# Attention and expert network on one core: the network folded into one 32x128 matrix a batch

## The chip, the cores and the metric

The kernel runs on one core of a Trainium2 chip. The metric is device time in microseconds of one execution. Engines: PE (TensorE: matmuls, transposes), DVE (VectorE), ACT (ScalarE), POOL (GpSimd) and SP (SyncE, which here issues the DMAs).

## The reference

For each of four batches of 11456 tokens with 128 features: 32 inducing vectors attend to all tokens, which gives `h` (32 rows), and the tokens attend to `h`. Then each token of the result goes to the one of eight experts whose vector it is nearest to, and through that expert's two-layer network (128 to 1024 to 128, ReLU), times the probability of that expert.

```python
def mab(q, kv):
    s = scale * (q @ kv.transpose(0, 2, 1))
    s = s - s.max(-1, keepdims=True)
    a = np.exp(s)
    a /= a.sum(-1, keepdims=True) + 1e-09
    return a @ kv
h = mab(I, x)
return mab(x, h).astype(np.float32)
...
    logits = xn @ en.T / tau
    expert_idx = np.argmax(logits, axis=1)
    ...
        h = np.maximum(x[mask] @ w1[e], 0.0)
        out[mask] = gate_w[mask, None] * (h @ w2[e])
```

A token's attended vector is a mix of the 32 rows of `h` with positive weights. Where the 32 rows' products with a column of `w1` are nearly equal, the sign of the mix is the sign of their sum, whatever the weights.

## The kernel before

A batch's tokens are cut into seven superblocks (`SBS`): five of four groups, one of two, one short one; a group is 512 tokens, four tiles of 128. A batch goes through two stages.

First stage (`stage1`): scores of the inducing vectors (`s1_pe`, four column strips of PE, L252), running maximum and exponentials (`s1_max` L265, `s1_exp` L282), transposes (`t1_pe` L297, `t1_copy` L303), products with the tokens into `h` (`h_pe` L310). `finish`, `table` and `guess` normalise `h`, make its table and choose the expert that most of the batch's tokens go to; `load_w` loads that expert's weights.

Second stage (`stage2`): scores against `h` (L252), copy (L478), transposes (L483), maximum, exponentials (L487 to L493), a split into float16 parts (`pst`, L496 to L499), transposes back into `pT` (L506). `norms` (L531, L542) gives squared lengths and logits, `gate` (L562 to L608) the factor of each token, which goes through memory (`gd`) to be spread over partitions (`gb`).

The network (`ffn`) goes over all groups of 512 tokens in eight chunks of the hidden layer. One step is one chunk:

```python
nc.tensor.matmul(ps[:, :w], lhsT=st.G[:K3, P * ch:P * ch + P], rhs=st.pT[k][:K3, w * t:w * t + w], start=True, stop=True)
nc.scalar.activation(hi[:, :w], ps[:, :w], AF.Relu)
nc.vector.scalar_tensor_tensor(lo[:, :w], ps[:, :w], 0.0, hi[:, :w], ALU.max, ALU.subtract)
```

and three matmuls with the second layer's parts `wh` and `wl` (L797, L798, L806). So a step is four matmuls of 512 columns, one ACT and one DVE instruction of 128x512. `G` is the first layer's weights times `h`. Attention runs as generators (`Clock`, `attention`) between the steps, 56 steps ahead of the network; the order is fixed by `FRAME` and the lags at the top of the file. Tokens of other experts than the batch's are redone in a loop at the end (`worklist` writes the list `items`; the loop reads it).

Of the kernel before, what the change touches and what calls it, by code (L numbers as in the profile page):

```python
# [83 lines left out]
def tile_attn_moe(ctx: ExitStack, tc: tile.TileContext, xT, xP, xR, indT, emb, tau, w1, w2, aux, outT):  # L84
    nc = tc.nc
    pool = lambda name, bufs, **kw: ctx.enter_context(tc.tile_pool(name=name, bufs=bufs, **kw))
    const = pool("const", 1)
# [13 lines left out]
    ps_acc = pool("ps_acc", 2, space=PSUM)
    ps_att = pool("ps_att", ATT_BUFS, space=PSUM)
    dram = pool("dram", 7, space=DRAM)
    keep = pool("keep", 1, space=DRAM)

    held = [0]

    def take():
        """A bank of attention's. It's given back (done) when all that reads it has been issued."""
        held[0] += 1  # L110
        assert held[0] <= ATT_BUFS
        return ps_att.tile([P, 512], F32, name="att")

    def done():
        held[0] -= 1

    def att():
        while held[0] >= ATT_BUFS:
            yield 1
        return take()  # L120

# [1 line left out]
    wz = const.tile([P, 512], F16, name="wz")  # L123
    nc.vector.memset(wz, 0.0)
    ident = const.tile([P, P], F32, name="ident")
    make_identity(nc, ident)
    ident16 = const.tile([P, P], F16, name="ident16")
    nc.vector.tensor_copy(ident16, ident)
    # sel4[(j, m), (r, m')] = 1 where m == m'
    sel4 = const.tile([P, 4, M], F32, name="sel4")  # L130
    for j in range(4):
        for r in range(4):
            nc.vector.tensor_copy(sel4[32 * j:32 * j + 32, r, :], ident[32 * j:32 * j + 32, 32 * j:32 * j + 32])
    ones = const.tile([P, P], F32, name="ones")
    nc.vector.memset(ones, 1.0)
    rev = const.tile([P, E], F32, name="rev")
    for e in range(E):
        nc.vector.memset(rev[:, e:e + 1], float(E - e))
    half = const.tile([P, 16], F32, name="half")
    nc.vector.memset(half, 0.5)  # L140

    indT_sb = const.tile([P, M], F32, name="indT_sb")
    nc.sync.dma_start(indT_sb, indT)
    emb_sb = const.tile([E, P], F32, name="emb_sb")
    itau = const.tile([P, 1], F32, name="itau")

    enT = const.tile([P, E], F32, name="enT")

    def load_small():
        nc.sync.dma_start(emb_sb, emb)  # L150
        nc.sync.dma_start(itau, tau.broadcast_to([P, 1]))
        nc.sync.dma_start(ax, aux)

    def experts():
        """The experts' vectors, normalised, transposed; in three parts."""
        nc.vector.reciprocal(itau, itau)
        esq = const.tile([E, P], F32, name="esq")
        ess = const.tile([E, 1], F32, name="ess")
        nc.scalar.activation(esq, emb_sb, AF.Square, accum_out=ess)
        nc.gpsimd.tensor_tensor(ess, ess, half[:E, 0:1], ALU.pow)  # L160
        yield
        nc.vector.tensor_scalar_add(ess, ess, 1e-6)
        nc.vector.reciprocal(ess, ess)
        nc.vector.tensor_scalar_mul(emb_sb, emb_sb, ess)
        yield
        tp = take()
        nc.tensor.transpose(tp[:, 0:E], emb_sb, ident[:E, :E])
        nc.vector.tensor_copy(enT, tp[:, 0:E])
        done()
        yield  # L170

    def squares(src, w):
        """The sums of the squares of src's rows."""
        junk = work.tile([P, 512], F32, name="junk")
        ss = small.tile([P, 1], F32, name="sq", bufs=6)
        nc.scalar.activation(junk[:, :w], src, AF.Square, accum_out=ss)
        return ss

    def pow2(sums):
        """A power of two, on every partition: times 2 ** -66 it takes the root of all the sums' sum  # L180
        to within [1 / 3, 1]."""
        ps = yield from att()
        for i, a in enumerate(sums):
            nc.tensor.matmul(ps[:, 0:1], lhsT=ones, rhs=a, start=i == 0, stop=i == len(sums) - 1)
        yield 1
        m1 = small.tile([P, 1], F32, name="m1")
        nc.vector.tensor_scalar_max(m1, ps[:, 0:1], 1e-30)
        done()
        # The exponent halved and negated: 2 ** (65 - (exponent + 1) // 2).
        m2 = small.tile([P, 1], F32, name="m2", bufs=4)  # L190
        nc.vector.tensor_scalar(m2.bitcast(I32), m1.bitcast(I32), 1, 0x7F800000, ALU.logical_shift_right, ALU.bitwise_and)
        nc.vector.tensor_scalar(m2.bitcast(I32), m2.bitcast(I32), 0x7F800000, None, ALU.bitwise_xor)
        return m2

    def scaled(m2, top, by, name):
        sc = small.tile([P, 1], F32, name=name, bufs=2)
        nc.vector.scalar_tensor_tensor(sc, m2, top * 2.0 ** -66, by, ALU.mult, ALU.mult)
        return sc

    def split_rows(dst, src, sc, odd):  # L200
        """dst[(hi, lo, hi, lo) x 32, w] of src (four equal blocks of rows) times sc. odd is sc in
        the blocks of lo and 0 in the others."""
        nc.scalar.activation(dst, src, AF.Copy, scale=odd)
        yield 1
        nc.vector.scalar_tensor_tensor(dst, src, sc, dst, ALU.mult, ALU.subtract)

    ax = const.tile([NB * E, 2 * NB * E + 2], F32, name="ax")
    onec = const.tile([P, 1], F32, name="onec")
    nc.vector.memset(onec, 1.0)

    par = const.tile([P, 1], F32, name="par")
    for q in range(4):
        nc.vector.memset(par[32 * q:32 * q + 32], float(q % 2))
    zcol = const.tile([P, 1], F16, name="zcol")
    for q in range(4):
        nc.vector.memset(zcol[32 * q:32 * q + 32], float(1 - q % 2))

    # What a second visit of a batch needs, and the experts that each batch's tokens go to.
    kT = keep.tile([NB, P, P], F32, name="kT")
# [897 lines left out]
```

## Time and profile before

| | |
|---|---|
| three runs | 841.62, 843.49 (median), 845.50 us |
| span of the profiled execution | 841.2 us |
| PE, DVE, ACT, POOL busy | 815.0 (97%), 702.9 (84%), 645.9 (77%), 182.7 us (22%) |
| DMA | 96.00 MB, mean 114 GB/s |

The span goes from the first to the last instruction of one profiled execution; no time of its own is given for that execution beside it, and the three runs lie 0.4 to 4.3 us above it. "Busy" is the union of an engine's instructions. Matmul ends are modelled, so distances between starts are the safer reading for PE.

### The profile page before, as it was taken

Reading aid. Unit: us, or ns where it says so; the run is one execution under the profiler, and the core shown is the slowest. Engines: PE = TensorE matmul, PEld = TensorE weight load, DVE = VectorE, ACT = ScalarE, POOL = GpSimd, SP = SyncE. Lnnn points to the kernel's source line nnn. Section 1 sums busy time; section 2 is a strip of 40 time slices with the busy share of each in tenths; the row PEclk is TensorE's granted clock in tenths of the full one; section 3 lists DMA queues with packets and bytes.
Section 4 is the critical chain, followed back from the end, with each engine's and each line's share of the span. In section 5 each row is a group of like instructions: output and inputs, shape, how many; then the busy total and the mean of one; then the engine's idle time right before and its main releaser. Section 6 shows DMA issues by size and latency. Waiting matters only on the chain.

```text
span 841.2 us, 15737 instructions
## 1 busy us (share of the span) xinstructions
PE 815.0 (97%) x5286; PEld 395.7 (47%) x5286; DVE 702.9 (84%) x1674; ACT 645.9 (77%) x1894; POOL 182.7 (22%) x388
## 2 busy tenths in 40 slices
PE   9899899999999999999999999999999999999994
PEld 5544445444544444444454444444454444444442
DVE  5587787987989889898898898888888988898983
ACT  4588768786887887877688878878688888888662
POOL 0034411221122222312022222222112222223100
PEclk9999999999999999999999999999999999999998
DMA  8534151422633324241663244132311122212221
GB/s 331 215 143 151 52 197 55 159 90 95 122 150 138 121 106 176 73 162 53 95 221 145 80 153 164 64 140 106 99 64 58 39 85 80 64 51 89 63 81 35
DMA packets 32091, 96.00 MB, mean 114 GB/s; under 512 B 5257, under 2 KB 7665, under 8 KB 27265
## 3 DMA queue, kind: packets, MB, share of 16 engines
q1 hardware_dynamic: 32000, 94.91, 33.1%
q8 instruction: 44, 0.72, 0.4%
q14 instruction: 47, 0.38, 0.2%
HBM read 70.84 MB, written 24.05 MB: 113 GB/s over the span
## 4 chain that ended last, share of the span: by engine, by line
PE 87%; DVE 3%; DMA 3%; ACT 3%; issue 1%; POOL 1%; SPq 1%; ACTq 0%; POOLq 0%
PE hps L783 18%; PE acc L797 17%; PE acc L806 17%; PE acc L798 17%; PE att L252 5%; PE att L531 3%; DMA w2t<-in_w 3%; PE att L310 2%; PE att L506 2%; PE att L297 1%; PE att L483 1%; ACT hi L785 1%; DVE lo L786 1%; ACT junk L542 1%; PE hps L874 1%
## 5 line engine op out<-in xcount | busy, mean ns | idle before, releaser
L786 DVE SCALAR_TENSOR_TENSOR lo<-hps,hi 128x512 f16<-128x512 f32 (+1 forms) x736 | 482.9, 671 | 77.9 <-ACT hi L785 71.7
L785 ACT ACTIVATE hi<-hps 128x512 f16<-128x512 f32 (+1 forms) x736 | 429.4, 589 | 110.0 <-PE hps L783 107.6
L783 PE MATMUL hps<-pT,G 96*128 96x512 f16 (+1 forms) x736 | 275.6, 375 | 1.4 <-DVE lo L786 0.7
L797 PE MATMUL acc<-hi,wh 128*128 128x512 f16 (+1 forms) x736 | 275.2, 374 | 0.3 <-DVE o L817 0.3
L806 PE MATMUL acc<-lo,wh 128*128 128x512 f16 (+1 forms) x736 | 273.6, 372 | 0.0
L798 PE MATMUL acc<-hi,wl 128*128 128x512 f16 (+1 forms) x736 | 273.4, 371 | 0.0
L562 POOL TENSOR_TENSOR nrm<-ss,half 128x4 f32<-128x4 f32 (+1 forms) x92 | 93.3, 1014 | 241.6 <-ACT junk L542 241.6
L542 ACT ACTIVATE junk<-att 128x128 f32<-128x128 f32 (+1 forms) x368 | 99.5, 286 | 15.8 <-PE att L531 11.9
L798 PEld LDWEIGHTS <-wl 128*128 128x128 f16 x736 | 72.2, 98 | 83.0 <-issue 1.8
L806 PEld LDWEIGHTS <-wh 128*128 128x128 f16 x736 | 70.7, 96 | 83.7 <-issue 0.4
L783 PEld LDWEIGHTS <-G 96*128 96x128 f16 x736 | 71.3, 97 | 81.3 <-issue 22.8
L797 PEld LDWEIGHTS <-wh 128*128 128x128 f16 x736 | 72.4, 98 | 58.9 <-issue 5.6
L542 ACT ACTIVATION_READ_ACCUMULATOR junk<-att 128x1 f32 (+1 forms) x368 | 78.7, 215 | 0.0
L817 DVE SCALAR_TENSOR_TENSOR o<-acc,cO,gb 128x512 f32<-128x512 f32 (+1 forms) x92 | 66.9, 727 | 0.9 <-DMA gb<-gd 0.4
L510 ACT COPY pT<-att 96x512 f16<-96x512 f16 (+1 forms) x90 | 48.9, 550 | 7.1 <-PE att L506 6.7
L531 PEld LDWEIGHTS <-pT 96*128 96x128 f16 (+1 forms) x368 | 29.6, 97 | 34.8 <-issue 13.2
L531 PE MATMUL att<-hst,pT 96*128 96x137 f16 (+1 forms) x368 | 45.1, 224 | 0.1
L497 POOL TENSOR_SCALAR pst<-pst 128x512 f16<-128x512 f16 (+2 forms) x28 | 15.2, 544 | 111.0 <-ACT pst L496 111.0
L506 PEld LDWEIGHTS <-pst 128*96 128x96 f16 (+1 forms) x368 | 26.2, 123 | 10.9 <-issue 1.7
L506 PE MATMUL att<-ident,pst 128*96 128x128 f16 (+1 forms) x368 | 28.1, 218 | 0.9 <-POOL pst L497 0.9
L252 PE MATMUL att<-xTt,hT 128*32 128x512 f32 (+1 forms) x192 | 28.0, 569 | 0.1
L543 DVE COPY raw<-att 128x27 f32<-128x27 f32 (+4 forms) x140 | 24.1, 174 | 3.8 <-ACT junk L542 2.3
(188 smaller groups left out, 635.3 us busy)
## 6 DMA issues: line engine op xcount, KB each, us to landing
gb<-gd SPq DMA_DIRECT2D x88, 256.0 KB, 3.4
out<-o SPq DMA_DIRECT2D x43, 512.0 KB, 4.4
xTt<-in_xT SPq DMA_DIRECT2D x20, 1024.0 KB, 7.1
xt<-in_xP SPq DMA_DIRECT2D x17, 1024.0 KB, 9.5
xTt<-in_xT SPq DMA_DIRECT2D x4, 512.0 KB, 11.4
w1t<-in_w SPq DMA_DIRECT2D x8, 256.0 KB, 3.0
w2t<-in_w SPq DMA_DIRECT2D x4, 512.0 KB, 5.8
xt<-in_xP SPq DMA_DIRECT2D x3, 512.0 KB, 12.4
```

The source lines that it names most:

```text
L252: nc.tensor.matmul(ps[32 * j:32 * j + 32, :ng * w].rearrange("p (g i) -> p g i", i=w), lhsT=lhsT, rhs=v[:, j], start=True, stop=True)
L506: nc.tensor.transpose(tp[:K3, w * t:w * t + w], pst[:w, 8 * c + t].rearrange("p q m -> p (q m)"), ident16[:w, :w])
L531: nc.tensor.matmul(v[:w, t - 3 * c], lhsT=st.pT[k][:K3, t * w:t * w + w], rhs=st.hst[:K3], start=True, stop=True)
L542: nc.scalar.activation(junk[:w, :C], v[:w, t, :C], AF.Square, accum_out=st.ss[k][:w, a:a + 1])
L562: nc.gpsimd.tensor_tensor(nrm[:, a:a + pw], ss[:, a:a + pw], half[:w, a:a + pw], ALU.pow)
L783: nc.tensor.matmul(ps[:, :w], lhsT=st.G[:K3, P * ch:P * ch + P], rhs=st.pT[k][:K3, w * t:w * t + w], start=True, stop=True)
L785: nc.scalar.activation(hi[:, :w], ps[:, :w], AF.Relu)
L786: nc.vector.scalar_tensor_tensor(lo[:, :w], ps[:, :w], 0.0, hi[:, :w], ALU.max, ALU.subtract)
L797: nc.tensor.matmul(acc[:, :w], lhsT=st.wh[:, ch], rhs=hi[:, :w], start=ch == 0, stop=False)
L798: nc.tensor.matmul(acc[:, :w], lhsT=st.wl[:, ch], rhs=hi[:, :w], start=False, stop=False)
L806: nc.tensor.matmul(acc[:, :w], lhsT=st.wh[:, ch], rhs=lo[:, :w], start=False, stop=ch == NCH - 1)
L817: nc.vector.scalar_tensor_tensor(o[:, a:a + w], acc[:, :w], st.cO, st.gb[k, t][:, :w], ALU.mult, ALU.mult)
```

## The change

The kernel is written anew. A superblock is now 1920 tokens (`SBT`), six to a batch, 24 in all (`NS`); its tokens are laid out as 15 blocks (`NQ`) of 4 x 32, so that four column strips of 32 partitions hold 480 columns (`W`). Everything is float32.

- Stage 1 (`stage1`): scores `s1`; exponentials `e1` with one shift for the whole batch, from the first superblock's maximum (`m1`, `shift`); `e1t` turns them with DVE's 32x32 transposes in place of PE transposes and copies; `h` takes 15 products into one bank held for the batch. For 14 of 24 superblocks the token-major tile is made from xT by 15 PE transposes (`xt`) and two copies on ACT (`xe`); the ten in `LOADED` load it.
- A batch's matrix (`finish`): `h` and its table `tab` (products with `h` itself and with the experts' vectors), the expert (`pick`), its weights (`loadw`), `G`, its transpose `GT`, its sum over the 32 rows; where the sum is positive, a hidden column counts as it stands (`gk`), otherwise as zero. `K` times the second layer gives the 32x128 matrix, four times over along partitions (`K4`).
- Stage 2 (`stage2`), for a pair of superblocks at a time: scores `s2`, their largest absolute value `am`, exponentials `e2`; `ud` multiplies, with eight 32x32 tiles of PE, the weights by the table for the squared lengths (`pu`) and by the logits' differences and ones (`pd`); `w` and `n2` (or `nn` on PE for three pairs) give squared lengths, `dt` turns the logits to tokens on partitions; the gate's chain runs on 30 columns for both superblocks (`ln`, `ex`, `r`, `fac`, `lg`, `el`, `S`, `pb`, `gf`); `F` spreads the factors with a DVE transpose, `eg` (POOL) multiplies the weights by them, `out` is the product with `K4` in four row strips into four banks, `oe` copies them on ACT, `store` writes.
- `checks` and `verdict` hold, per batch, the largest score, the smallest margin of a column's sum, the largest logit difference and others against bounds; `n_left` is 0 or 4, and a loop at the end redoes that many batches in full, with all eight experts.
- The order on every engine comes from `Plan.run`: operations with an engine, a duration, a position (`pos` plus the table `OFF`) and buffers (`SLOTS`) are started in the order of positions as engine, inputs and slots allow, and written down in that order.

The heart of the diff (`-` of the network's step, `+` of the new functions):

```diff
-            nc.tensor.matmul(ps[:, :w], lhsT=st.G[:K3, P * ch:P * ch + P], rhs=st.pT[k][:K3, w * t:w * t + w], start=True, stop=True)
-            nc.scalar.activation(hi[:, :w], ps[:, :w], AF.Relu)
-            nc.vector.scalar_tensor_tensor(lo[:, :w], ps[:, :w], 0.0, hi[:, :w], ALU.max, ALU.subtract)
...
+LOADED = [2, 3, 6, 7, 9, 13, 15, 19, 21, 22]
+LAG = 7.0
+OFF = dict(F=-1.19, G=0.36, GT=-2.11, K=-1.75, K4c=-0.68, Kc=-1.89, am=1.12, ck1=1.09, ck2=-1.62, ck4=-0.41, ck5=2.55, cn1=2.18, e1=0.35, e1t=1.23, eg=1.08, el=1.26, en1=2.0, en2=-0.6, en4=0.06, ex=0.18, fac=0.48, h2=0.35, hde=2.41, hsb=-0.45, marg=0.51, n2=2.08, nc=3.36, nn=-2.43, oe=1.4, out=-2.34, pb=1.0, pick=-2.18, shb=-2.85, shd=-2.69, small=2.93, stb=1.85, stc=-2.37, tabs=-2.27, zc=0.97, zr=1.51)
...
+GATE = -2.2113
+OUT = 3.5374
+N2_PE = (18, 20, 22)
...
+SLOTS = dict(ps=8, xT=10, xP=3, xD=2, E1=2, E1T=2, E2=3, Wp=2, DT=2, F=2, E2g=2, o=3, gs=2, b=3, w=1, k=1)
...
+    def scores(ps, lhsT, xt):
+        v = xt.rearrange("c (q j i) -> c j q i", j=4, i=32)
+        return [mm(ps[32 * j:32 * j + 32, :W].rearrange("p (q i) -> p q i", i=32), lhsT, v[:, j]) for j in range(4)]
...
+        add(f"e1t {g}", {"DVE": 0.58}, lambda e: [nc.vector.transpose(ap(e1t), ap(e1))], [e1], [e1t], pos)
+        def h(e):
+            out = []
+            for q in range(NQ):
+                c = (q + k * NQ) % 4
+                out.append(mm(ap(bt.hacc)[32 * c:32 * c + 32, 0:C], ap(e1t)[:, 32 * q:32 * q + 32], ap(x)[:, q],
+                              start=k == 0 and q < 4, stop=k == K - 1 and q >= NQ - 4))
+            return out
...
+        def gk(e):
+            return [v.scalar_tensor_tensor(kt("Gk"), t("sm")[:, 0].unsqueeze(2).broadcast_to([P, 8, M]), 0.0, kt("GT"), ALU.is_gt, ALU.mult)]
...
+        def kmm(e):
+            return [mm(ap(pk)[32 * (f % 4):32 * (f % 4) + 32, 0:C], kt("Gk")[:, f], wt("w2")[:, f], start=f < 4, stop=f >= 4) for f in range(8)]
...
+            def ud(e, pu=pu, a=a):
+                out = []
+                for j in range(4):
+                    r, r2 = slice(32 * j, 32 * j + 32), slice(32 * ((j + 1) % 4), 32 * ((j + 1) % 4) + 32)
+                    out.append(mm(ap(pu)[r, :W], t("tab")[r, 0:M], ap(e2)[r, a]))
+                    out.append(mm(ap(pd)[r2, :W], t("tD")[r, a], ap(e2)[r, a], start=a == 0, stop=a == 1 and g0 not in N2_PE))
+                return out
...
+            add(f"w {g}", {"DVE": 0.66}, lambda e, pu=pu, a=a: [v.tensor_tensor(ap(wp)[:, a], ap(pu)[:, :W], ap(e2)[:, a], ALU.mult)], [pu, (e2, a)], [(wp, a)], pos)
...
+            add("n2 " + nm, {"DVE": 1.1}, lambda e: [v.tensor_reduce(fl2(u("n2")), ap(wp).rearrange("p a (q i) -> p (a q) i", i=32), AX.X, ALU.add, apply_transpose=True)],
...
+        add("dt " + nm, {"DVE": 0.66}, lambda e: [v.transpose(ap(dt_).rearrange("p q m -> p (q m)"), ap(pd)[:, :W])], [pd], [dt_], pos)
...
+            add(f"F {g}", {"DVE": 0.58}, lambda e, a=a, f=f: [v.transpose(ap(f).rearrange("p (q i) -> p q i", i=32), u("gf")[:, a].unsqueeze(2).broadcast_to([P, NQ, 32]))],
...
+            add(f"eg {g}", {"POOL": 1.55}, lambda e, a=a, f=f, e2g=e2g: [gp.tensor_tensor(ap(e2g), ap(e2)[:, a], ap(f), ALU.mult)], [(e2, a), f], [e2g], pos)
+            po = [Buf("ps", 2), Buf("ps", 2)]
+            def out(e, e2g=e2g, po=po):
+                return [mm(ap(po[j // 2])[:, j % 2, :W], t("K4")[32 * j:32 * j + 32], ap(e2g)[32 * j:32 * j + 32]) for j in range(4)]
...
+    n_left = nc.values_load(ni, min_val=0, max_val=NB)
...
+    with tc.For_i(0, n_left, 1) as b:
...
+            for e in range(E):
+                nc.sync.dma_start(wr, w1[e])
+                nc.sync.dma_start(w2p, w2[e])
+                for f in range(8):
+                    mm(bank[f % 2][:, :GW], wr[:, P * f:P * f + P], yg[:, e])
+                    nc.scalar.activation(hid, bank[f % 2][:, :GW], AF.Relu)
+                    mm(bank[7][:, :GW], w2p[:, f], hid, start=e == 0 and f == 0, stop=e == E - 1 and f == 7)
```

What the change leaves on PE in the middle of the program. Before, the network's step over and over (`hps` is a chunk's bank, `acc` the output's, each matmul behind its weight load):

```order
L797 LDWEIGHTS wh
L797 MATMUL acc<-hi,wh 128x512
L798 LDWEIGHTS wl
L798 MATMUL acc<-hi,wl 128x512
L806 LDWEIGHTS wh
L806 MATMUL acc<-lo,wh 128x512
L783 LDWEIGHTS G
L783 MATMUL hps<-pT,G 128x512
```

After, in the middle too; all banks are called `psum`. `xT,ind` is `s1`, `xD,E1T` is `h`, `ident,xT` is `xt`, `E2g,K` is `out`, `w,hd` is `G`, `v,back` is `pb`, `E,tab` and `E,tD` are the first of the eight products of `ud`:

```order
L301 MATMUL psum<-xT_69,ind 32x480 x4
L301 MATMUL psum<-st_194,nsc 128x1
L301 MATMUL psum<-xD_79,E1T_83 32x128 x15
L393 MATMUL psum<-ident,xT_69 128x128 x8
L301 MATMUL psum<-E2g_94,K_122 128x480 x4
L301 MATMUL psum<-w_152,hd_128 32x256 x4
L301 MATMUL psum<-v_103,back 128x30
L650 MATMUL psum<-ident,chk_123 7x128
L301 MATMUL psum<-xT_70,ind 32x480 x4
L301 MATMUL psum<-E_84,tab_129 32x480
L301 MATMUL psum<-E_84,tD_130 32x480
```

The four matmuls of a step are gone, and operations of three batches and of both stages stand next to each other, each of another tile shape.

On DVE, before, in the middle (`lo` is the hidden layer's low part, the rest is attention and gate):

```order
L786 SCALAR_TENSOR_TENSOR lo<-hps,hi 128x512
L565 RECIPROCAL r<-r 128x16
L786 SCALAR_TENSOR_TENSOR lo<-hps,hi 128x512 x2
L499 SCALAR_TENSOR_TENSOR pst<-d,pst 128x16x32
L786 SCALAR_TENSOR_TENSOR lo<-hps,hi 128x512 x2
L573 RECIPROCAL nrm<-nrm 128x16
```

After, in the middle (`E1T` is `e1t`, `Wp` is `w`, `n` is `n2`, `r`, `den`, `v` and `gf` belong to the gate, `rm` to the checks):

```order
L566 TENSOR_REDUCE n_138<-Wp_87 128x30
L416 STREAM_TRANSPOSE E1T_83<-E_80 128x480
L533 TENSOR_REDUCE am_131<-psum 128x1 x2
L550 TENSOR_TENSOR Wp_87<-psum,E_85 128x480
L588 RECIPROCAL r_99<-s_98 128x30
L588 TENSOR_TENSOR r_99<-psum,r_99 128x30
L593 TENSOR_TENSOR den_102<-r_99,z_101 128x30
L593 RECIPROCAL den_102<-den_102 128x30
L611 TENSOR_REDUCE rm_137<-lg_105 128x8
L603 TENSOR_REDUCE v_103<-ex_106 128x30
```

The `lo` instruction is gone, and its place is taken by transposes, reductions and the gate's pieces, which read what PE, ACT and POOL made for another pair.

More of the change, by code (lines that the diff above doesn't have):

```diff
@@ L6 @@
 from concourse import mybir
+from concourse._compat import with_exitstack
 from concourse.masks import make_identity
-from concourse._compat import with_exitstack
 F32 = mybir.dt.float32
-F16 = mybir.dt.float16
 I32 = mybir.dt.int32
@@ L101, in tile_attn_moe @@
[L101 to L219, printed above, removed]
-    kst = keep.tile([NB, P, HW], F16, name="kst")
-    kcH = keep.tile([NB, P, 1], F32, name="kcH")
-    items = keep.tile([NB * E, 2], I32, name="items")
@@ L286, in s1_sum @@
-    def s1_sum(st, k):
-        if k:
-            z = small.tile([P, 1], F32, name="zs", bufs=NSB)
-            nc.vector.scalar_tensor_tensor(z, st.z1, st.fix[k], st.zk[k], ALU.mult, ALU.add)
-            st.z1 = z
-        else:
-            st.z1 = st.zk[k]
-    def t1_pe(st, k, tp):
-        g0, ng, w = SBS[k]
-        for g in range(ng):
-            nc.tensor.transpose(tp[:w, 128 * g:128 * g + 128], st.s1[k][:, w * g:w * g + w], ident)
-        st.pt1[k] = tp
-    def t1_copy(st, k, eng=None):
-        g0, ng, w = SBS[k]
-        pt = work.tile([P, 4, P], F32, name="pt", bufs=3)
-        (eng or nc.scalar.copy)(pt[:w, :ng].rearrange("p g c -> p (g c)"), st.pt1.pop(k)[:w, :128 * ng])
-        st.pt[k] = pt
@@ new lines, in tile_attn_moe, with tiles @@
+    keep = ctx.enter_context(tc.tile_pool(name="keep", bufs=1))
+    main = ExitStack()
+    sb = main.enter_context(tc.tile_pool(name="sb", bufs=1))
+    psp = main.enter_context(tc.tile_pool(name="psp", bufs=1, space=PSUM))
+    psum = psp.tile([P, 8, 512], F32, name="psum")
+    def tiles(kind, shape, dt=F32):
+        return [sb.tile(shape, dt, name=f"{kind}{i}") for i in range(SLOTS[kind])]
+    T = dict(
+        xT=tiles("xT", [P, SBT]), xP=tiles("xP", [P, NQ, C]), xD=tiles("xD", [P, NQ, C]),
+        E1=tiles("E1", [P, W]), E1T=tiles("E1T", [P, W]), E2=tiles("E2", [P, 2, W]), Wp=tiles("Wp", [P, 2, W]),
+        DT=tiles("DT", [P, NQ, 32]), F=tiles("F", [P, W]), E2g=tiles("E2g", [P, W]), o=tiles("o", [P, SBT]))
@@ new lines, in tile_attn_moe @@
+    for t in T["k"]:
+        t["ei"] = sb.tile([P, 8], U32, name="ei")
+    const = lambda name, shape: keep.tile(shape, F32, name=name)
+    ident, ind, ones, iota = const("ident", [P, P]), const("ind", [P, M]), const("ones", [P, P]), const("iota", [P, E])
+    sel = const("sel", [P, 5, M])
+    fwd, back = const("fwd", [P, P]), const("back", [P, P])
+    len2 = const("len2", [P, 2, 32])
+    en, enu, itau, ess, embT = const("en", [P, E]), const("enu", [P, E]), const("itau", [P, 1]), const("ess", [P, E]), const("embT", [P, E])
@@ new lines, in tile_attn_moe, with ap, copy, mm @@
+    plan = Plan()
+    add = plan.add
+    made = []
+    def ap(b, part=None):
+        if b.kind == "ps":
+            return psum[:, b.slot] if b.n == 1 else psum[:, b.slot:b.slot + b.n]
+        t = T[b.kind][b.slot]
+        return t[part] if part is not None else t
+    ENG = dict(PE=nc.tensor, ACT=nc.scalar, DVE=nc.vector, POOL=nc.gpsimd, SP=nc.sync)
+    def copy(e, out, in_):
+        return nc.scalar.copy(out, in_) if e == "ACT" else ENG[e].tensor_copy(out, in_)
+    def mm(out, lhsT, rhs, start=True, stop=True):
+        return nc.tensor.matmul(out, lhsT=lhsT, rhs=rhs, start=start, stop=stop)
@@ new lines, in tile_attn_moe, with load_small @@
+    cbuf, cnb = Buf("cst"), Buf("cst")
+    enb, tb, sb_ = Buf("cst"), Buf("cst"), Buf("cst")
+    add("ind", {"ACT": (0.6, 16e3)}, lambda e: [nc.scalar.dma_start(ind, indT)], [], [cnb], -9.9)
+    def load_small(e):
+        return [nc.scalar.dma_start(emb_sb, emb), nc.scalar.dma_start(itau, tau.broadcast_to([P, 1]))]
+    add("small", {"ACT": (1.0, 5e3)}, load_small, [], [tb], -9.8)
+    eps0, eps_ = Buf("ps"), Buf("ps")
+    add("en0", {"PE": 0.1}, lambda e: [nc.tensor.transpose(ap(eps0)[:, 0:E], emb_sb, ident[:E, :E])], [tb, cbuf], [eps0], -4)
@@ new lines, in tile_attn_moe @@
+    for g in range(NS):
+        stage1(g)
+        if g % K == K - 1:
+            finish(g // K)
+    for g in range(0, NS, 2):
+        stage2(g)
+        if g % K == K - 2:
+            checks(g // K)
+    add("verdict", {"DVE": 1.2}, verdict, [(flb, b) for b in range(NB)], [(flb, "n")], NS + LAG)
+    for op in plan.ops:
+        op.bufs = [b for b in op.bufs if b.kind in SLOTS]
+    order = plan.run()
+    with tc.manual_schedule():
+        nc.scalar.preload_act_table_set("natural_log_exp_and_others")
+        constants()
+        hist, last = {}, {}
+        for op in order:
+            res = []
+            for key in (op.reads, op.writes):
+                out = []
+                for b, part in key:
+                    if b.kind == "ps":
+                        out += [("ps", s) for s in range(b.slot, b.slot + b.n)]
+                    elif b.kind in SLOTS:
+                        out.append((b.kind, b.slot, part))
+                    else:
+                        out.append((b, part))
+                res.append(out)
+            reads, writes = res
+            writes += [k for k in reads if k[0] == "ps"]
+            deps = []
+            for key in reads + writes:
+                w, r = hist.setdefault(key, [None, []])
+                if w is not None:
+                    deps.append(w)
+            for key in writes:
+                deps += hist[key][1]
+            deps = [d for d in dict.fromkeys(deps) if d is not op]
+            for key in writes:
+                hist[key] = [op, []]
+            for key in reads:
+                hist[key][1].append(op)
+            op.insts = op.f(op.engine)
+            touches = any(b.kind == "ps" for b in op.bufs)
+            op.group = touches
+            if touches:
+                others = [d for d in deps if d.group]
+                for n, x in enumerate(op.insts):
+                    if op.engine in last:
+                        kept = [last[op.engine].ins]
+                    else:
+                        kept = []
+                    tc.declare_no_dep(x.ins, group="psum", keep=kept + [y.ins for y in op.insts[:n]] + [y.ins for d in others for y in d.insts], reason="banks")
+                    last[op.engine] = x
+                    tc.add_to_no_dep_group("psum", x.ins)
+                for d in others:
+                    if d.engine != op.engine:
+                        tc.add_manual_dep(op.insts[0].ins, d.insts[-1].ins.name,
+                                          mybir.DependencyInfo(mybir.DependencyClass.Sync, mybir.DependencyReason.DATA), reason="data")
```

1319 lines of the change are left out of this document (533 added, 786 removed).

## The prediction

> **What bounds the kernel now.** I read the page's busy times and its chain first, then the groups by form, then the windows.
>
> ```profile
> span 841.2 us, 15737 instructions
> ...
> PE 815.0 (97%) x5286; PEld 395.7 (47%) x5286; DVE 702.9 (84%) x1674; ACT 645.9 (77%) x1894; POOL 182.7 (22%) x388
> ...
> PE 87%; DVE 3%; DMA 3%; ACT 3%; issue 1%; POOL 1%; SPq 1%; ACTq 0%; POOLq 0%
> PE hps L783 18%; PE acc L797 17%; PE acc L806 17%; PE acc L798 17%; PE att L252 5%; PE att L531 3%; DMA w2t<-in_w 3%; PE att L310 2%; PE att L506 2%; PE att L297 1%; PE att L483 1%; ACT hi L785 1%; DVE lo L786 1%; ACT junk L542 1%; PE hps L874 1%
> ```
>
> TensorE is busy for 97% of the span and carries 87% of the chain that ended last; 69 points of it are the four matmuls of the experts' network (L783, L797, L798, L806). The other engines' share of the network:
>
> ```profile
> L786 DVE SCALAR_TENSOR_TENSOR lo<-hps,hi 128x512 f16<-128x512 f32 x704 | 472.6, 685 | 71.8 <-ACT hi L785 65.7 <-ACT gT L608 0.3
> L785 ACT ACTIVATE hi<-hps 128x512 f16<-128x512 f32 x704 | 419.4, 600 | 100.7 <-PE hps L783 100.0
> ```
>
> ```profile
> 10.00:20.00 10.00, 9.55 (x138) 6.65 (x137) 6.82 (x20) 5.16 (x14) 0.24 (x1) 1.00 1.01 420
> 400.00:600.00 200.00, 198.24 (x1298) 96.11 (x1298) 172.13 (x402) 159.58 (x472) 44.72 (x94) 1.00 0.39 125
> ```
>
> In mid-kernel PE runs 198.24 of 200 us beside a DVE at 86% and an ACT at 80%. In the first stage, from 10 to 20 us, the loads reach 420 GB/s with the DMA engines full. PE's granted clock is 1.00 in both.
>
> **What goes.** The whole network: 69% of the chain, 580 us of 841, with 473 us of DVE and 419 us of ACT behind it. Its place is taken by one 32-row product per superblock. Out go also the attention's transposes and the gate's trip through memory. What is left is too different to subtract from 841, so I add up the new kernel from prices. A sum for each engine shows which one is the bound.
>
> **PE.** The timeline of PE gives starts, and the distance between starts is the price.
>
> ```profile
> 5.14 1.08 PE L252 MATMUL acc<-xTt,indT_sb 128*32 128x256 f32 x8 [0.24 <-DMA xTt<-in_xT]
> ...
> 13.18 1.07 PE L252 MATMUL acc<-xTt,indT_sb 128*32 128x512 f32 x8
> 14.06 1.06 PE L310 MATMUL att<-xt,pt 128*32 128x128 f32 x32
> 15.04 2.09 PE L874 MATMUL hps<-ident,xTt 128*128 128x128 f32 x16
> 16.98 0.60 PE L297 MATMUL att<-ident,s 128*128 128x128 f32 x4
> ...
> 29.27 1.08 PE L310 MATMUL att<-xt,pt 128*32 128x128 f32 x32
> 30.82 0.38 PE L420 MATMUL att<-selr,hj 128*128 128x1 f32 x2 [0.47 <-DVE hj L320]
> 31.07 0.47 PE L421 MATMUL att<-sel,hj 128*128 128x128 f32 x2
> ...
> 32.08 0.64 PE L252 MATMUL att<-xTt,hT 128*32 128x256 f32 x8
> ...
> 36.34 2.28 PE L657 MATMUL acc<-w1t,hT 128*128 128x512 f32 x4 [0.50 <-DMA w1t<-in_w]
> 38.45 0.50 PE L184 MATMUL att<-sq,ones 128*128 128x1 f32 x4
> ...
> 51.03 0.38 PE L798 MATMUL acc<-hi,wl 128*128 128x512 f16 x1
> 51.25 0.38 PE L806 MATMUL acc<-lo,wh 128*128 128x512 f16 x1
> 51.56 1.05 PE L252 MATMUL att<-xTt,indT_sb 128*32 128x512 f32 x2
> 52.53 0.39 PE L783 MATMUL hps<-pT,G 96*128 96x512 f16 x1
> 52.85 1.06 PE L252 MATMUL att<-xTt,indT_sb 128*32 128x512 f32 x6
> 53.85 0.39 PE L797 MATMUL acc<-hi,wh 128*128 128x512 f16 x1
> ```
>
> A float32 matmul shows as two records. Four score products of 512 columns on four column strips take 0.88 us (13.18 to 14.06); one strip alone takes 0.97 (51.56 to 52.53) and three together 1.00, so strips run side by side. At 480 columns four take 0.83 us. Sixteen h products take 0.98, so 15 take 0.92. A 128x128 transpose is 1.94 / 16 = 0.121 us. A small product is 0.25 (30.82 to 31.07). A score product starts 0.31 us behind a float16 one (51.25 to 51.56), where another float16 one starts after 0.22 (51.03 to 51.25), so a change of shape costs some 0.09 us.
>
> `out` (32 rows by 128 columns, four row strips) and `ud` (eight 32x32 tiles) have no row. They lie between 0.83 us each (all side by side) and one after another: 3.3 us for `out`, 6.6 for `ud`. I take 0.83, since the nearest row, four column strips, runs so.
>
> Per superblock: four groups at 0.83 (`s1`, `s2`, `ud`, `out`), `h` 0.92, five changes of shape 0.45: 4.7 us, and 113 for 24. Added to that: 210 transposes 25, 67 small products 17, the experts' `G` and `K` 4, `nn` 5. **PE: 164 us.**
>
> The Trainium skill speaks against part of this: "TensorEngine Tiling (Array Packing)", section "Restrictions and Gotchas", says that different row tiles cannot access one PSUM bank at the same time, and `ud` sends four row strips into one bank. Its page "TensorE: Matmul & The Clock Gate" (last table) has four 32-row tiles 3.07 times as fast as one after another; no row here shows a row strip. By the first rule PE would have 59 us more (second rival).
>
> **DVE, ACT, POOL.**
>
> ```profile
> L490 DVE TENSOR_TENSOR d<-att,mx 128x512 f32<-128x512 f32 x20 | 13.6, 682 | 0.0
> L578 POOL TENSOR_TENSOR lg<-raw,fac 128x128 f32<-128x128 f32 x20 | 8.1, 406 | 1.6
> L282 ACT ACTIVATE s<-att,nb 128x512 f32<-128x512 f32 x15 | 10.2, 680 | 0.0
> L596 DVE TENSOR_REDUCE se<-ex 128x16 f32<-128x128 f32 x20 | 5.5, 273 | 0.1
> L875 ACT COPY xt<-hps 128x512 f32<-128x512 f32 x10 | 5.3, 589 | 0.0
> L598 DVE RECIPROCAL se<-se 128x16 f32<-128x16 f32 x20 | 5.0, 250 | 0.5
> L282 ACT ACTIVATION_READ_ACCUMULATOR s<-att,nb 128x1 f32 x21 | 4.2, 199 | 0.0
> L303 DVE COPY pt<-att 128x512 f32<-128x512 f32 x4 | 2.8, 690 | 2.4 <-PE att L297 2.4
> L490 DVE TENSOR_TENSOR d<-att,mx 128x256 f32<-128x256 f32 x4 | 1.7, 419 | 0.0
> L478 ACT COPY s<-att 128x256 f32<-128x256 f32 x4 | 1.5, 372 | 0.8 <-PE att L252 0.8
> L578 POOL TENSOR_TENSOR lg<-raw,fac 128x64 f32<-128x64 f32 x4 | 1.2, 295 | 0.3
> ```
>
> DVE: 682 and 419 ns for 512 and 256 columns make 0.16 us and 1.03 ns a column, 0.65 us for 480. There are 110 of that size (`e1t`, `w`, `F` 24 each, `am` and `m1` 26, `dt` 12): 72 us. The 32x32 transposes among them (60) have no row: from 0.4 us (two elements a step would halve the columns' part) to 0.7 (L303); I take 0.65, by the row that is nearest in size and in moving a whole tile (L303). Nine `n2` over 960 columns at 1.14: 10. A pair's gate has eight small ones of 0.2 to 0.4 us (L598, L596), 2.2 us, by 12: 26. A batch's matrix and checks are some 38 small ones, 7.5 us, by 4: 30. **DVE: 138 us**, 123 to 141 by the transposes' ends.
>
> ACT: 589 and 372 ns make 0.85 ns a column. 28 token copies (1024 or 896 columns) 27 us, 48 output copies of 960 columns at 0.97 46, 24 `e1` at 0.65 + 0.20 with the four split ones 24, 24 `e2` at 0.65 16, gates and rest 13. **ACT: 126 us.** POOL: (406 - 295) / 64 = 1.73 ns a column gives 1.0 us for each of 24 `eg`, and 1.4 for a pair's rest: 42 us, off the path.
>
> **DMA.**
>
> ```profile
> q1 hardware_dynamic: 32000, 94.91, 33.1%
> ...
> out<-o SPq DMA_DIRECT2D x43, 512.0 KB, 4.4
> ...
> items<-li SPq DMA_DIRECT2D x1, 0.2 KB
> ```
>
> xT is loaded once as before (23.5 MB), ten of 24 token-major tiles again (9.8), four batches' weights (4.2), and 23.5 are stored: 61 MB. At the 420 GB/s of the second window that is 145 us, under PE. The Trainium skill ("DMA: Bandwidth & Descriptors", Specifications) limits a core's share of memory to about 358 GB/s, by which it would be 170 us; this trace's 420 decides.
>
> **The sum.** Head: the first batch's h needs eight tiles, 7.9 MB. Half of one has landed at 5.14 us; the other 7.4 MB at 420 GB/s land at 22.7. From the last h product to the next scores the old kernel takes 32.08 - 29.27 = 2.8 us; one product and one copy more make it 4.3. So second stages begin at 27 us. By then PE has done eight `s1` (7), six `h` (6) and the transposes of four superblocks (7): 21 of 164. The other 143 us run as PE ran in the second window, 99% busy, because DVE and ACT stand to PE now as then (138 / 164 = 84%, 126 / 164 = 77%, against 86% and 80%): 144 us, to 171. When the stage-one work has run out, some seven superblocks are left with only second stages; there PE has 2.9 us each and DVE 3.9 (`am`, `w`, `F` 0.65 each, half of `n2` and `dt` 0.9, half a gate 1.1), so 7 us are added: 178. After PE's last product come a copy or two (1.9 us), a store of 1 MB (4.4 us for half of that, some 6) and the branch on the checks, some 2 us: 188. The page's span is 841.2 and the runs' median 843.49, 2 us more, partly scatter; I add 1. **189 us.**
>
> Its own range: 174 if the changes of shape are hidden (-11) and cheap transposes let DVE keep up at the end (-4) to 207 (PE at 90% in the middle, +16, and all else as taken).
>
> **Rivals.**
> *DMA is the bound.* For: 94.91 MB took 33.1% of 841.2 us, 341 GB/s of busy engines; at that 61 MB take 179 us, and loads wait for one of ten xT tiles while stores stand behind them on SP's one queue. Against: 420 GB/s in the full window. 5 + 179 + the last superblock's chain and store, some 20: **204 us**.
> *Row strips that share a bank go one after another.* `ud` then takes 3.3 us, two groups of four, each pair side by side: 24 x 2.5 = 59 more on PE: **248 us**. Against: each strip writes other partitions of the bank.
> *The engines wait for each other.* A pair's gate crosses engines some fifteen times, and eight banks serve everything (an `out` takes four). If PE is busy 75% of the middle, 143 / 0.75 = 191: **236 us**; at 85%, 213. Against: the same loads of DVE and ACT left PE full.
> *Slower than before: the checks fail.* The loop at the end then redoes all four batches for all experts (`n_left` is 0 or 4): 4 x 32 pieces of 358 columns, each with 128 matmuls. A float32 matmul of 512 columns takes 1.05 us (36.34 to 38.45 for two), 0.74 for 358: 4 x 32 x 128 x 0.74 us = **12 ms**. One failed condition decides. Against: before's work list was written (`items`) and never read, so in every batch all tokens go to the chosen expert; and by the reference's arithmetic on a draw of its inputs the signs' bound is 0.00013 and the smallest margin 0.0015.
>
> **How the numbers follow.** Forecast 0.62, DMA 0.12, waits between engines 0.14, row strips 0.10, checks fail 0.02. The range of 80% goes from 174 to 226: it holds the forecast's case nearly whole, DMA's, and half of the waits'; row strips, checks and the worst waits stay outside. 0.5% is about what this kernel's runs can tell from no change (841.62 to 845.5). All cases but the last are far faster: 0.97; same 0.01; slower 0.02.
>
> **What would show it.** Right: no instruction of the last loop, PE about 85% busy over the span, `ud` and `out` groups of about 0.9 us between starts, DVE 32x32 transposes near 0.65 us, first scores on `hd` near 27 us, DMA share below 0.85 in the middle. Wrong: `ud` starts spread over 3 us, a DMA share near 1.0 after 60 us, or PE waiting for ACT's copies of `o`.

## The result and the profile after

The changed kernel takes 203.14 us (median of 202.38, 202.72, 203.57 and 203.60), the kernel before 843.90 us on the same chip: a ratio of 0.2411 [0.2401, 0.2420]. The prediction was 189 us with a range of 174 to 226. The profiled execution took 202.38 us, its span is 200.6. Where an experiment's executions differed by more than 1.5%, only the undisturbed ones are used below.

The page of the kernel after: busy times, rows of the 40 slices, and what DMA moved.

```profile
span 200.6 us, 5485 instructions
...
PE 173.8 (87%) x2151; PEld 84.6 (42%) x2151; DVE 138.3 (69%) x402; ACT 116.2 (58%) x204; POOL 54.5 (27%) x138
...
PE   0799999999999999999999997999997979873430
...
PEclk9969999999999999999999999999999999999555
DMA  6899999999986299999877999245459833589563
...
DMA packets 9983, 61.38 MB, mean 306 GB/s; under 512 B 1368, under 2 KB 1376, under 8 KB 9952
```

Windows of the kernel after: window and its length; busy us of PE, weight loads, DVE, ACT and POOL; granted clock, DMA share, GB/s.

```profile
20.00:50.00 30.00, 29.83 (x442) 16.86 (x431) 16.84 (x46) 15.73 (x31) 1.58 (x5) 1.00 1.02 416
50.00:80.00 30.00, 29.85 (x423) 16.64 (x415) 27.16 (x85) 18.36 (x37) 7.83 (x13) 1.00 0.79 281
80.00:110.00 30.00, 29.95 (x368) 14.76 (x364) 23.66 (x66) 19.91 (x35) 8.52 (x16) 1.00 0.90 353
110.00:140.00 30.00, 28.99 (x395) 14.15 (x388) 24.72 (x65) 21.02 (x38) 9.13 (x15) 1.00 0.71 274
140.00:160.00 20.00, 18.56 (x220) 6.71 (x222) 17.71 (x54) 13.34 (x21) 5.68 (x8) 1.00 0.72 264
160.00:180.00 20.00, 16.79 (x180) 5.35 (x172) 16.51 (x44) 11.80 (x21) 10.96 (x20) 1.00 0.55 226
180.00:200.60 20.60, 6.36 (x36) 1.83 (x28) 7.05 (x31) 7.86 (x10) 3.27 (x5) 0.64 0.60 245
...
0.00:32.63 32.63, 25.92 (x319) 16.98 (x319) 8.79 (x30) 14.55 (x27) 7.56 (x59) 0.95 0.93 370
32.63:192.20 159.57, 147.87 (x1833) 67.59 (x1832) 129.52 (x372) 99.85 (x176) 46.98 (x79) 0.98 0.77 300
192.20:200.60 8.40, 0.00 (x0) 0.00 (x0) 0.00 (x0) 1.82 (x2) 0.00 (x0) 0.50 0.46 181
```

From 20 to 140 us PE is busy for 118.6 of 120 us. DMA runs full from 10 to 50 us, then between 0.71 and 0.90 up to 160. The holes on PE lie in the first 20 us and after 140. In the fullest stretch, 50 to 80, DVE is busy for 91% beside PE's 99.5%.

PE's timeline in the kernel after. Starts count; the second figure is the length of a run of records.

```profile
4.71 1.94 PE L393 MATMUL psum<-ident,xT 128*128 128x128 f32 x8 [4.71 <-DMA xT<-in_xT]
...
6.78 1.81 PE L301 MATMUL psum<-xT,ind 128*32 128x480 f32 x8
...
11.62 1.66 PE L301 MATMUL psum<-xT,ind 128*32 128x480 f32 x8
...
13.73 2.58 PE L393 MATMUL psum<-ident,xT 128*128 128x128 f32 x15
16.24 1.01 PE L301 MATMUL psum<-xT,ind 128*32 128x480 f32 x8
...
24.39 1.85 PE L393 MATMUL psum<-ident,xT 128*128 128x128 f32 x15
...
32.63 1.01 PE L301 MATMUL psum<-xT,hd 128*32 128x480 f32 x8
...
81.59 1.82 PE L301 MATMUL psum<-xT,hd 128*32 128x480 f32 x16
83.33 1.09 PE L301 MATMUL psum<-E2g,K 32*128 32x480 f32 x8
84.35 0.41 PE L301 MATMUL psum<-n,fwd 128*128 128x30 f32 x2
84.69 1.07 PE L301 MATMUL psum<-xP,E1T 128*32 128x128 f32 x30
85.69 0.58 PE L301 MATMUL psum<-E,tab 32*32 32x480 f32 x1
...
85.74 0.58 PE L301 MATMUL psum<-E,tD 32*32 32x480 f32 x1
86.12 0.56 PE L301 MATMUL psum<-E,tab 32*32 32x480 f32 x1
...
86.17 0.56 PE L301 MATMUL psum<-E,tD 32*32 32x480 f32 x1
86.66 1.07 PE L301 MATMUL psum<-xD,E1T 128*32 128x128 f32 x30
```

Eight products of `ud` start within 0.05 us (the first and the last of the eight are shown, 85.69 and 85.74), their second records within 0.05 us again (86.12 to 86.17), and the next operation 0.97 us after the first: all eight run side by side, in two banks. `out` takes 1.02 us (83.33 to 84.35), two sets of `s2` 1.74.

Groups of the kernel after, the operations that had no row before:

```profile
L298 ACT COPY o<-psum 128x960 f32<-128x960 f32 x48 | 44.5, 961 | 22.9 <-PE psum L301 20.5
L618 POOL TENSOR_TENSOR E2g<-E,F 128x480 f32<-128x480 f32 x24 | 29.0, 1210 | 42.7 <-PE psum L301 24.3
...
L416 DVE STREAM_TRANSPOSE E1T<-E 128x480 f32<-128x480 f32 x24 | 15.9, 666 | 9.2 <-PE psum L301 4.7
...
L616 DVE STREAM_TRANSPOSE F<-gf 128x480 f32<-128x480 f32 x24 | 15.3, 653 | 0.2
```

### The profile page after: what moved, and what is told of

Read it like the earlier page. It is cut to its first block, busy times and chain, and to the rows that moved or that the text cites. A ratio compares the mean times of both kernels' runs of the same rounds, so it can differ in the third digit from the quotient of the medians.

```text
span 200.6 us, 5485 instructions
## 1 busy us (share of the span) xinstructions
PE 173.8 (87%) x2151; PEld 84.6 (42%) x2151; DVE 138.3 (69%) x402; ACT 116.2 (58%) x204; POOL 54.5 (27%) x138
## 5 line engine op out<-in xcount | busy, mean ns | idle before, releaser
L298 ACT COPY o<-psum 128x960 f32<-128x960 f32 x48 | 44.5, 961 | 22.9 <-PE psum L301 20.5
L618 POOL TENSOR_TENSOR E2g<-E,F 128x480 f32<-128x480 f32 x24 | 29.0, 1210 | 42.7 <-PE psum L301 24.3
L301 PE MATMUL psum<-E2g,K 32*128 32x480 f32 x192 | 27.9, 651 | 7.4 <-POOL E2g L618 2.4
L393 PE MATMUL psum<-ident,xT 128*128 128x128 f32 x210 | 29.4, 288 | 4.7 <-DMA xT<-in_xT 4.7
L298 ACT COPY xP<-psum 128x1024 f32<-128x1024 f32 (+1 forms) x28 | 26.5, 960 | 12.1 <-PE psum L393 11.6
L393 PEld LDWEIGHTS psum<-ident,xT 128*128 128x128 f32 x210 | 24.5, 149 | 11.9 <-issue 7.4
L301 PE MATMUL psum<-xT,ind 128*32 128x480 f32 x192 | 26.7, 606 | 0.1
L301 PE MATMUL psum<-E,tab 32*32 32x480 f32 x192 | 24.2, 572 | 0.0
L301 PE MATMUL psum<-E,tD 32*32 32x480 f32 x192 | 24.2, 572 | 0.0
L301 PE MATMUL psum<-xT,hd 128*32 128x480 f32 x192 | 23.5, 576 | 0.2 <-ACT xP L298 0.2
L416 DVE STREAM_TRANSPOSE E1T<-E 128x480 f32<-128x480 f32 x24 | 15.9, 666 | 9.2 <-PE psum L301 4.7
L597 POOL TENSOR_TENSOR lg<-DT,den 128x240 f32<-128x240 f32 x12 | 7.6, 637 | 16.8 <-DVE den L593 14.1
```

The source lines that it names most:

```text
L298: return nc.scalar.copy(out, in_) if e == "ACT" else ENG[e].tensor_copy(out, in_)
L301: return nc.tensor.matmul(out, lhsT=lhsT, rhs=rhs, start=start, stop=stop)
L393: return [nc.tensor.transpose(ap(tp)[:, (q - q0) // 4, 128 * ((q - q0) % 4):128 * ((q - q0) % 4) + 128], v(q), ident) for q in range(q0, q1)]
L416: add(f"e1t {g}", {"DVE": 0.58}, lambda e: [nc.vector.transpose(ap(e1t), ap(e1))], [e1], [e1t], pos)
L597: add("lg " + nm, {"POOL": 0.8}, lambda e: [gp.tensor_tensor(u("lg"), dv(), u("den").rearrange("p a q -> p q a").unsqueeze(3).broadcast_to ...
L618: add(f"eg {g}", {"POOL": 1.55}, lambda e, a=a, f=f, e2g=e2g: [gp.tensor_tensor(ap(e2g), ap(e2)[:, a], ap(f), ALU.mult)], [(e2, a), f], [e ...
```

## The experiments

The theory: PE is the bound, and the 14 us above the forecast are mostly PE work and waits that the sum left out at both ends. Rivals: DMA is the bound; DVE or ACT is; the order of `Plan.run` leaves room. Times are set against 203.2 us, the change's own.

**PE doubled in one place.** Each set of `s2` is issued twice.

```diff
-scores(ap(ps), t("hd")[:, 0:32], ap(xt))
+scores(ap(ps), t("hd")[:, 0:32], ap(xt)) + scores(ap(ps), t("hd")[:, 0:32], ap(xt))
```

> Every superblock's second-stage scores are computed twice on PE, in the same order: 24 x 0.87 us = 21 us more of PE. PE is the bound (busy 128.6 of the 130 us from 20 to 150): 203 becomes 220 to 224, since only the last few superblocks lie where PE has gaps. Rival, the loads and stores are the bound (DMA share 0.98 from 30 to 60 us): at most 208. Rival, the chains between the engines are the bound: 205 to 212.

222.78 us, ratio 0.2642 [0.2614, 0.2671]: 19.6 us more for 24 x 0.87 = 20.9 us of added products. PE's time goes straight into the end.

**DVE and ACT doubled in one place,** the order unchanged: `F` twice, and `e2` twice.

```diff
-[v.transpose(ap(f)..., u("gf")[:, a]...)]
+[v.transpose(ap(f)..., u("gf")[:, a]...), v.transpose(ap(f)..., u("gf")[:, a]...)]
```

> The DVE transpose that spreads the factors is done twice: 24 x 0.65 us = 15.7 us more of DVE, in the same order. PE is the bound: hidden up to 150 us, and on the path for the last four to six superblocks, 205 to 208. Rival, the chains between the engines are the bound: 211 or more.

216.28 us: 13.1 more for 24 x 0.653 = 15.7 us of DVE. The theory's 205 to 208 is wrong here; the time lies where its rival had put it (211 or more).

> The second-stage exponentials are done twice on ACT: 24 x 0.65 us = 15.8 us more of ACT, in the same order. PE is the bound: 204 to 207. Rival, the chains between the engines are the bound: 211 or more.

207.61 us, 0.2462 [0.2447, 0.2478]: 4.4 more for 24 x 0.659 = 15.8 us of ACT. It is just above the theory's 207. ACT has slack, though not enough to hide all.

**Is it the stale order?** `F` twice again, and the planner is told of it (1.24 us in place of 0.58).

> The spreading transpose is done twice as in the earlier run (216 to 220), but the planner is told of it (1.24 instead of 0.58 us), so the order fits the longer work. If DVE's time as such is what costs (DVE and PE both full in places), 214 or more. If it was the order that no longer fitted, 205 to 210.

219.09 us, 0.2599 [0.2590, 0.2608]: planning with the true price doesn't help, and 15.9 us more for 15.7 us of DVE is a slope near one too. Two of its windows, and PE's wait for `eg`:

```profile
50.00:80.00 30.00, 27.72 (x356) 15.04 (x348) 26.98 (x80) 17.13 (x32) 7.61 (x12) 1.00 0.59 210
...
160.00:172.00 12.00, 8.51 (x71) 2.75 (x72) 9.17 (x30) 4.69 (x8) 3.04 (x3) 0.57 0.52 208
```

```profile
PE psum L301 <- POOL E2g L618: 8.7, 4, 3.1
```

In the kernel after, the same wait:

```profile
PE psum L301 <- POOL E2g L618: 2.4, 1, 2.4
```

PE loses 2.1 us between 50 and 80, where DVE is 90% busy, and at the end it waits 8.7 us for `eg` where it waited 2.4; all four waits come after 150 us. `F` is a link of the chain `gf`, `F` (both on DVE), `eg` (POOL), `out` (PE), and no `out` of the pair can go ahead of it. The holes then cost more than their length: from 160 to 172 us the granted clock is 0.57, and the same 2151 products keep PE busy for 178.8 us in place of 173.8. So some 5 of the 15.9 us are slower products. DVE, busy for 91% of the change's fullest window, is close behind PE in the middle, and longer work on it reaches the end. Whether it is DVE's time as such or the longer chain of a pair stays open: no run lengthened DVE outside that chain.

**No tile loaded twice.** All 24 token-major tiles are made on PE.

```diff
-LOADED = [2, 3, 6, 7, 9, 13, 15, 19, 21, 22]
+LOADED = []
```

> No token-major tile is loaded again: ten more are made by 15 PE transposes (10 x 1.8 us = 18 us more of PE, 19 us more of ACT) and 9.8 MB less are loaded (23 us less of DMA at 420 GB/s). The order is planned anew. PE is the bound: 215 to 222. Rival, DMA is the bound: 203 or less.

224.65 us, 0.2664 [0.2652, 0.2677]. The page and a window of it:

```profile
PE 195.9 (88%) x2301; PEld 100.5 (45%) x2301; DVE 142.7 (64%) x405; ACT 133.7 (60%) x221; POOL 54.4 (24%) x138
...
DMA packets 8545, 51.58 MB, mean 232 GB/s; under 512 B 1208, under 2 KB 1216, under 8 KB 8512
```

```profile
20.00:50.00 30.00, 30.00 (x422) 19.33 (x414) 12.44 (x39) 17.79 (x29) 0.70 (x3) 1.00 0.53 201
```

With 9.8 MB less to move, and DMA half empty from 20 to 50 us, the kernel is 21.4 us slower, somewhat more than the theory's 215 to 222; PE has 22.1 us more. DMA isn't the bound.

**More tiles loaded.** Three more than ten, on top of the version of the last experiment of this document, "Stores first" (201.55 us in the same set of runs).

> The same, with three more token-major tiles loaded (8, 14, 20) in place of 45 PE transposes: 5.5 us less of PE, 2.9 MB or 7 us more of DMA; the order is planned anew. If PE alone is the bound of the middle, 5 us less than the run above; if DVE or the loads stand right behind PE, 0 to 2 us less, or more.

211.03 us, 0.2505 [0.2495, 0.2515]: 9.5 slower, where less work on PE should have helped. The windows of this kernel, and then of the one it is made from:

```profile
80.00:110.00 30.00, 28.16 (x346) 13.29 (x342) 24.17 (x71) 18.00 (x32) 8.57 (x16) 1.00 0.95 352
110.00:140.00 30.00, 27.59 (x353) 11.09 (x352) 22.48 (x57) 19.01 (x35) 8.54 (x13) 0.94 0.97 351
140.00:160.00 20.00, 16.04 (x184) 7.45 (x191) 17.97 (x58) 11.83 (x21) 6.81 (x11) 1.00 0.54 206
```

```profile
80.00:110.00 30.00, 29.95 (x365) 14.52 (x364) 23.76 (x64) 20.73 (x37) 8.72 (x17) 1.00 0.91 349
110.00:140.00 30.00, 28.82 (x392) 14.07 (x394) 24.72 (x68) 21.02 (x37) 8.90 (x14) 1.00 0.73 279
140.00:160.00 20.00, 18.73 (x221) 6.55 (x213) 17.80 (x52) 12.51 (x20) 5.69 (x8) 1.00 0.70 266
```

The DMA share goes from 0.73 to 0.97 between 110 and 140, and PE loses 5.7 us from 80 to 160. But of its waits there only 0.8 us end on a load; the longest (1.6 and 1.5 us) end on DVE. A new set also gives a new order, whose table was made for the old set; how much belongs to the loads and how much to the order stays open.

**The order's table.** All offsets zero:

```diff
-OFF = dict(F=-1.19, G=0.36, ...)
+OFF = {}
-GATE = -2.2113
+GATE = 0.0
```

> The table of positions that shifts the operations (OFF, GATE) is set to zero; same work, same costs, same buffers, planned by plain positions. If the engines are kept full by the number of buffers and the work alone, as the prediction argued from the old kernel's shares, 203 to 208. If the tuned order is what keeps PE full, 215 or more.

212.6 and 215.0 us, 0.2534 [0.2516, 0.2551]: the same instructions in another order cost 10.6 us more. That lies between the two forecasts: the order matters more than 203 to 208 would have it, and less than 215 or more. The table is worth 5%.

**The two ends.** First the control, the change itself, in the set of runs of the next three:

> The changed kernel as it is, for comparison on the same chip: 202 to 204.

203.31 us, 0.2402 [0.2393, 0.2410].

*Head:* PE is kept busy by eight products of zeros before the first tile comes, and the experts' vectors no longer stand ahead of the first shift.

```diff
+    add("fill", {"PE": 0.3}, lambda e: [mm(ap(fb), wz[:, 0:P], wz) for _ in range(8)], [cbuf], [fb], -99)
-    add("en5", {"DVE": 1.0}, experts5, [eps_, (enb, 1), sb_], [(enb, 0), (enb, 2)], -4)
+        if g == 0:
+            add("en5", {"DVE": 1.0}, experts5, [eps_, (enb, 1), sb_, tb, (bs[0].st, ("nb", 0))], [(enb, 0), (enb, 2)], 2)
```

> Two edits at the start: eight idle matmuls on PE before the first tokens are there, so that its clock is up, and the experts' vectors are finished behind the first shift on DVE, so that the first maximum no longer waits for the load of tau. PE's gap from 8.6 to 10.4 us and some 2.5 us of half-rate work go: 198.5 to 200. Rival, the head is bound by the loads: 202 to 203, with the first token products waiting for DMA.

201.87 us, 0.2389 [0.2377, 0.2402]: 1.4 less, not 3 to 5, and the intervals of the two ratios overlap. Its PE timeline:

```profile
1.18 3.22 PE L304 MATMUL psum<-wz 128*128 128x512 f16 x8 [1.18 <-DVE wz L262]
...
4.84 1.07 PE L397 MATMUL psum<-ident,xT 128*128 128x128 f32 x8 [0.44 <-DMA xT<-in_xT]
...
22.70 1.01 PE L304 MATMUL psum<-xT,ind 128*32 128x480 f32 x8 [1.20 <-DMA xT<-in_xT]
...
31.90 1.01 PE L304 MATMUL psum<-xT,hd 128*32 128x480 f32 x8
```

The first eight transposes take 1.07 us in place of 1.94, so PE is ahead of the loads, and now waits for them: the last tile of the batch is there at 22.70, as forecast, and the scores on `hd` begin only 0.7 us earlier than in the change. What remains of the head is 9.2 us of work behind the last load. The edit also keeps the granted clock (the third column from the end) up a little later. The windows from 12 to 15 us, of the change and then of this run, show it:

```profile
12.00:15.00 3.00, 3.00 (x16) 1.77 (x9) 0.96 (x6) 1.28 (x3) 0.44 (x3) 0.50 1.01 425
```

```profile
12.00:15.00 3.00, 2.86 (x49) 1.36 (x50) 1.37 (x4) 2.71 (x6) 0.44 (x3) 1.00 1.02 428
```

*Tail:* the verdict goes after the last gate, and DVE takes one of the two copies of `o` of each of the last two superblocks.

```diff
-[(flb, "n")], NS + LAG)
+[(flb, "n")], NS + LAG + 9)
-BY_DVE = ()
+BY_DVE = ((22, 1), (23, 1))
```

> Two edits at the end: the verdict (13 small DVE instructions, 3.3 us) stands behind the last spreading transpose instead of ahead of it, and DVE makes one of the two output copies of the last two superblocks. The last out product starts 2 us earlier and the copies overlap: 199.5 to 201. Rival, the end is bound by the stores or by the branch that waits for the verdict: 202.5 to 203.5.

203.26 us, 0.2404 [0.2399, 0.2409]: nothing. In the change the verdict stands between the last two `F` (the first and the last of its instructions are shown):

```profile
184.85 0.12 DVE L664 TENSOR_SCALAR fw<-fl 1x4 f32<-1x4 f32 x1
...
188.06 0.14 DVE L677 CAST ni<-fw 1x1 int32<-1x1 f32 x1
188.13 0.66 DVE L616 STREAM_TRANSPOSE F<-gf 128x480 f32<-128x480 f32 x1
...
190.21 1.98 PE L301 MATMUL psum<-E2g,K 32*128 32x480 f32 x8 [1.88 <-POOLq L748]
192.30 1.82 ACT L298 COPY o<-psum 128x960 f32<-128x960 f32 x2 [2.04 <-issue]
```

Moved, the verdict stood ahead of DVE's copies instead: its last instruction is at 190.56 us, the copies start at 190.93, and the last two stores are issued from 192.15 on, where the change issues them at 190.28 and 194.15. SP still read `n_left` ahead of them. The wait only changed its place.

> Both edits of the start and both of the end. If they add up: 195.5 to 198. If the shorter head only moves the waiting into the middle: 200 or more.

202.28 us, 0.2399 [0.2388, 0.2410]: no more than the head's part.

*Stores first:* head and late verdict, all copies on ACT, and `n_left` is read after the last store is issued.

```diff
+        n_left = nc.values_load(ni, min_val=0, max_val=NB)
     main.close()
...
-    n_left = nc.values_load(ni, min_val=0, max_val=NB)
```

> The edits of the start as before; at the end the verdict stands behind the last spreading transpose, all copies stay on ACT, and SP issues the last two stores ahead of reading the verdict's number (before, it read the number first, so the stores stood behind it). Against the version with the edits of the start alone (201.9): if the read of the verdict held the last stores, 198.5 to 200; if the stores' own time is the end, 201 to 202.

201.55 us (201.38 to 201.74), 0.2389 [0.2385, 0.2394]. This is the fastest version by its median, and no execution of it reaches the control's lowest (202.11), which comes from another set of runs; the two ratios' intervals just touch. Against the head alone the 0.3 us are within the scatter. Its last `out` ends 3.3 us earlier than the change's and its span only 1.0: the two last stores, 1.9 MB, now go one behind the other.

## Why the prediction was right, and where it was not

The mechanism was right: PE bounds the kernel (99% busy from 20 to 140 us, and a slope near one in the two experiments that add work to it), `ud` and `out` run side by side, DMA is not the bound, and no instruction of the last loop ran. The slope alone would not show it, since doubling `F` gave as steep a one. The sign "DMA share below 0.85 in the middle" did not hold everywhere: it is 0.90 from 80 to 110 us. The time is 14.1 us above the sum. By its steps:

| step | predicted us | measured us |
|---|---|---|
| start to first scores on `hd` | 27 | 32.6 |
| from there to the end of the last product | 151 | 159.6 |
| of it PE busy | 143 | 147.9 |
| of it PE idle before 140 us | 1 | 1.2 |
| of it PE idle after 140 us | 7 | 10.5 |
| last product to the end of the span | 10 | 8.4 |
| outside the span | 1 | 1.8, and 0.8 to the median |

- **The head, "one product and one copy more make it 4.3".** This is the step that failed. The last tile did land at 22.7, but behind it stood its own scores, transposes (1.8 us), three `h`, two `s1` of the next batch and the table's small products: 9.2 us in the experiment where PE stood waiting for that tile. The sum had counted such work (21 us of PE, though its pieces 7, 6 and 7 make 20) and let it run before the load.
- **PE: 164 us, measured 173.8.** Four pieces, each small. Of the 67 small products, 51 stand 0.31 to 0.34 us apart (84.35 to 84.69) and not 0.25, the rest, transposes, some 0.20: together some 3 us. `ud` and `out` at 0.97 and 1.02 with their change of shape, against 0.92: with `s2`'s 0.87 some 2 us. The slow start, 3 us: first 1.94 and 1.81 us for what takes 1.07 and 1.01, then, at the granted clock of 0.50 behind a hole of 1.79 us, 1.66 against 1.01 for the second `s1` (11.62) and 2.58 against 1.85 (13.73). At the end two `out` at half clock, 1.98 against 1.09: 1.8 us.
- **The shapes without a row** came out where they were taken: transposes on DVE 0.65 to 0.68 us (0.65), `out` and `ud` near 0.83 and a change of shape. DVE's sum was 138 and is 138.3, though `am` and `m1` are 28 instructions and not 26; ACT's 126 and 116.2. POOL's was 42 and is 54.5: `eg` takes 1.21 us and not 1.0, which is 5 us, and some 7 us are the constants made in the first 8.6 us, which the sum left out. `eg` is in the last pairs' chain, where PE waits 2.4 us for it.
- **"Because DVE and ACT stand to PE now as then."** The 99% came, the reason doesn't hold: the same shares with the table at zero leave the kernel 10.6 us slower, and 15.7 us more on DVE cost 13 or more. Such shares allow a full PE; this one needs the tuned order as well, so that the 99% came out is in part luck.
- **The tail.** DVE was named as its bound, with 7 us. From 160 to 180 us PE is at 84% and DVE at 83%, so neither is full, which leaves the gate's chain over all engines; this is argued, not tested by itself. The verdict stands in that chain, but without it (in "Stores first", which has the head's edit too) the last `out` ended 3.3 us earlier and the span only 1.0.
- **The range.** 189 and 16 make 205, not the 207 given for PE at 90%; the range's ends do not hang on it.
- **The rivals.** DMA at 341 GB/s: its 204 us is nearer to the time than the forecast's 189, but the loads ran at 416 GB/s from 20 to 50 us, and less load made the kernel slower, so the nearness is chance. Row strips one after another, 248 us: 0.97 us for eight products shows that they don't go so. There the trace contradicts the Trainium skill, "TensorEngine Tiling (Array Packing)", "Restrictions and Gotchas": four row strips wrote one bank at the same time, each to partitions of its own. Waits between engines, 213 to 236: not in this order; the untuned one takes 212.6 to 215.0 us, and how much of that is waiting was not taken apart.

## What to carry to other kernels

Where a sum over engines gives the bound, add what it can't hold: the work that stands behind the last load of the first result, and the chain of the last tile; here they were 9 of 14 us. An engine at 70% of the span can still be the second bound: look at its share in the fullest window and at the chain it is a link of before calling its time free. A small check at the end stands in the queue of every engine that it uses. Moving it on one engine alone gained nothing, and behind the last stores in all of them 0.3 us, within the scatter: look first at what else the end waits for, here two stores one behind the other.
